# Two matmuls for three in the last token tile of six expert blocks, with earlier output copies and earlier turns, in an attention + mixture-of-experts kernel

## The chip, the cores and the metric

The kernel runs on one core of a Trainium2 chip. The metric is the device time of one launch in microseconds (us); the number quoted for a kernel is the median of several runs. The profile is of one more execution, taken by the hardware profiler. Engines are named as the profile names them: PE (TensorE matmul), PEld (its weight load, which runs beside the matmuls), DVE (VectorE), ACT (ScalarE), POOL (GpSimd), SP (SyncE, which here only issues transfers).

## The reference, cut to what matters

```python
x = attention(q, k, v, f_logit)            # gated linear attention -> 3072 tokens x 384
logits = x @ w_gate + log1p(exp(x @ w_noise)) * noise
top2   = the two experts (of 8) with the highest logits, softmax weights top2_w
for e in range(8):                          # mixture of experts
    mask = tokens that chose e
    h = np.maximum(x[mask] @ w1[e], 0.0)    # 384 -> 1024
    out[mask] += top2_w[mask] * (h @ w2[e]) # 1024 -> 384
xn  = out / rms(out) * rms_g                # second feed-forward, all tokens
y   = (silu(xn @ w_gate2) * (xn @ w_val2)) @ w_out   # 384 -> 1536 -> 384
```

All products are wanted at float32 accuracy. The kernel gets it by splitting each operand into a rounded part and a remainder, both in float32r, and adding three matmuls: rounded x rounded, rounded x remainder, remainder x rounded (`three`, L673).

## The kernel before, in words

The first 150 us are the attention. Then comes the expert stream, 22 blocks one after the other on PE: eight blocks with the first 384 tokens of each expert, eight with the rest of each expert (the experts ranked by how many tokens they hold, so that the sizes are known when the program is built: 476, 448, 428, 416, 408, 396, 392 and 384 rows), and six blocks of the second feed-forward.

An expert block has 8 units; a unit is 128 hidden columns. Its first product (`l1`) has the tokens as the moving operand: 9 matmuls of N columns into one PSUM bank named h (two banks, taken in turn). ACT makes the rounded part `hhi` of the relu (L801), DVE the remainder `hlo` (L802). Its second product (`l2`, `down_product`) has the hidden values as the stationary operand, one tile of 128 tokens at a time, and 384 columns of w2 as the moving one: three matmuls per token tile, accumulated over the 8 units in one PSUM bank per tile (`acc`). PE's order is written out by hand: l1 of unit f, then l2 of unit f-2. So a block of 428 tokens has tiles of 128, 128, 128 and 44 rows, and the last takes three matmuls like the others.

After a block's last unit, `post` copies each tile's bank to SBUF (`y`, L816 on DVE for odd tiles, L818 on ACT for even ones) and SP stores it. The next block's l2 needs the same banks.

The token rows of a block come by gathers on POOL (`fetch`, L770; four of 32 rows a tile, into six buffers `xg`), then `turn` transposes them on DVE (`xt`, L781) and splits them into `xhi` (ACT, L668) and `xlo` (DVE, L669). A table gives the units in which this is issued: tile 0 to 3 at 5, 4, 3 and 2 units before the block starts, the gathers two units ahead of it and at most two in a unit. Weights come by SP transfers into two buffers `raw`; ACT and DVE split them (`whi` L209, `wlo` L210). The second feed-forward's weights are 64-bit numbers and take more steps (`cv`: L178 on ACT, L179, L180 and L182 on DVE; `whi` L205; `wlo` on POOL, L206). On ACT, DVE, POOL and SP a scheduler sets the order from priorities; only PE's is by hand.

Of the kernel before, what the change touches and what calls it, by code (L numbers as in the profile page):

```python
# [9 lines left out]
F32 = mybir.dt.float32  # L10
F32R = mybir.dt.float32r
# [4 lines left out]
AF = mybir.ActivationFunctionType  # L16
OP = mybir.AluOpType
# [4 lines left out]
P = 128  # L22
# [5 lines left out]
def tile_gated_attention_moe_ffn(  # L28
# [18 lines left out]
    nc = tc.nc  # L47
    B, HP, _, S = f_logit.shape
    DM = v.shape[2]
# [22 lines left out]
    main = ExitStack()  # L72
# [193 lines left out]
    late = {}  # L266
    mark = [None, None]
# [426 lines left out]
            V.tensor_tensor(r, r, t, op=OP.mult)  # L694

    class Block:
        pass


    def behind(on=True):  # L700
# [15 lines left out]
    def down_product(b, key, f, hh, rows, only=None):  # L716
        whi, wlo = wts_of[key + (f // 2,)]
        for i, r in enumerate(rows):
            if only not in (None, i):
                continue  # L720
            c = slice(i * P, i * P + r)
            three(b.acc[i][:r], whi[:, f % 2], wlo[:, f % 2], hh[0][:, c], hh[1][:, c],
                  f == 0, f == b.units - 1, False)

    def x_tiles(b, n):
# [1 line left out]
        b.xlo = xs_.tile([P, KD, 512], F32R, name="xlo")  # L727

    def h_tiles(n):
        return [late["h"].tile([P, 512], F32R, name=nm) for nm in ("hhi", "hlo")]  # L730

    def moe_block(e, t0, N, pid):

# [3 lines left out]
        b = Block()  # L737
        rows = [min(P, N - o) for o in range(0, N, P)]
        b.units = FM // P
        b.uses = lambda f: [("up", pid, f // 2)], lambda f: [("down", pid, f // 2)]  # L740
        b.cost = 9 * max(N, 256) / 2400, len(rows) * 3 * DM / 2400

# [50 lines left out]
        def l1(f):  # L793
            whi, wlo = wts_of["up", pid, f // 2]
            c = slice((f % 2) * P, (f % 2 + 1) * P)
            p = bank("h")
            for j in range(KD):
                three(p[:, :N], whi[:, j, c], wlo[:, j, c], b.xhi[:, j, :N], b.xlo[:, j, :N],
                      j == 0, j == KD - 1, True)
            hhi, hlo = h_tiles(N)  # L800
            mark[0] = nc.scalar.activation(hhi[:, :N], p[:, :N], AF.Relu).ins  # L801
            mark[1] = nc.vector.scalar_tensor_tensor(  # L802
                hlo[:, :N], p[:, :N], 0.0, hhi[:, :N].bitcast(F32), op0=OP.max,
                op1=OP.subtract).ins
            return hhi, hlo

        def l2(f, hh):
            if f == 0:
# [3 lines left out]
        def post():  # L812
            for i, r in enumerate(rows):
                y = late["h"].tile([P, DM], F32, name="y")
                if i % 2:
                    nc.vector.tensor_copy(y[:r], b.acc[i][:r])  # L816
                else:
                    nc.scalar.activation(y[:r], b.acc[i][:r], AF.Copy)  # L818
                o = (t0 + i) * P
                to = yd.rearrange("(e s) d -> e s d", e=E)[:, o:o + r]  # L820
                if t0 == 0:
                    nc.sync.dma_start(to[e], y[:r])
                    o += e * CAPA
                    nc.sync.dma_start(ya[o:o + r, :], y[:r])
                else:
                    nc.sync.dma_start(to[bass.ds(expert_of(e), 1)].rearrange("o s d -> (o s) d"),
                                      y[:r])
# [4 lines left out]
    def ffn_block(bi):  # L832
        b = Block()
# [46 lines left out]
        def l1(f):  # L880
            c = slice((f % 2) * P, (f % 2 + 1) * P)
            ps = []
            for nm, use in (("gate", "h"), ("val", "t")):
                whi, wlo = wts_of[nm, f // 2]
                p = bank(use)
                for j in range(KD):
                    three(p, whi[:, j, c], wlo[:, j, c], b.xhi[:, j], b.xlo[:, j],
                          j == 0, j == KD - 1, True)
                ps.append(p)
            sg = late["f"].tile([P, 512], F32, name="sg")  # L890
            nc.scalar.activation(sg, ps[0], AF.Sigmoid)  # L891
            nc.vector.tensor_tensor(sg, ps[0], sg, op=OP.mult)  # L892
            nc.vector.tensor_tensor(sg, ps[1], sg, op=OP.mult)  # L893
            hhi, hlo = h_tiles(512)
            mark[0] = nc.scalar.activation(hhi, sg, AF.Copy).ins  # L895
            mark[1] = nc.vector.tensor_tensor(hlo, sg, hhi.bitcast(F32), op=OP.subtract).ins
            return hhi, hlo

        def l2(f, hh):
            if f == 0:  # L900
# [40 lines left out]
    for pid in range(2 * E):  # L941
        r = pid - E if pid >= E else None
# [63 lines left out]
    start = [0]  # L1006
# [7 lines left out]
    for i in range(1, len(blocks)):  # L1014
        b = blocks[i]
        if i < NM:
            where = (-5, -4, -3, -2)
        else:
            where = (-50, -48, -46, -44, -42, -4, -3, -2) if i == NM else \
                (-9, -8, -7, -6, -5, -4, -3, -2)  # L1020
        for u, fn in zip(where, b.turns):
            side.setdefault(start[i] + u, []).append(fn)
        skip = GIVEN if i == 1 else 0
        for u, fns in zip(where, b.fetches):
            fns, skip = fns[skip:], max(0, skip - len(fns))
            if i > NM:
                side.setdefault(start[i] + u - 2, []).extend(fns)
            else:
                wanted += [(start[i] + u - 2, fn) for fn in fns]
# [458 lines left out]
```

## Time and profile before

| | |
|---|---|
| median of 3 runs | 1075.31 us (1072.07 to 1076.23) |
| the profiled execution | 1068.86 us, its span 1067.0 us |
| mean granted TensorE clock | 0.994 |
| busy: PE, PEld | 1029.9 us (97%), 935.8 us (88%) |
| busy: DVE, ACT, POOL | 669.1 us (63%), 482.5 us (45%), 300.0 us (28%) |
| chain that ended last | PE 83%, DVE 7%, ACT 3%, DMA 3% |

The span runs from the first to the last instruction; the execution's own time lies 1.9 us above it. A matmul's record is longer than the distance to the next one, because matmuls are pipelined: what a matmul costs is read from one start to the next, not from its mean length. The attention ends at about 150 us, the last expert block at about 590 us.

### The profile page before, as it was taken

To read this page: it belongs to the slowest core of one execution; us is meant where nothing else is said; L and a number is where in the kernel's file an instruction comes from. 1 tells how busy PE (TensorE), PEld (TensorE's weight loads), DVE (VectorE), ACT (ScalarE), POOL (GpSimd) and SP (SyncE) were. 2 spreads that over 40 slices of the span, in tenths; PEclk is the share of its full clock that TensorE was granted. 3 is DMA by queue.
4 is the path that set the end of the run, shared out by engine and by line. 5 is a ranking of instruction groups with operands and counts; after the bars stand their busy time and mean duration, and the time that the engine had idled before them with its cause. 6 is when DMAs were issued, how large, how long until landed. Compare 5 with 4: busy or idle time off the path is not lost.

```text
span 1067.0 us, 17429 instructions
## 1 busy us (share of the span) xinstructions
PE 1029.9 (97%) x6497; PEld 935.8 (88%) x6497; DVE 669.1 (63%) x1473; ACT 482.5 (45%) x1048; POOL 300.0 (28%) x318
## 2 busy tenths in 40 slices
PE   8898899999999999999999999999999999999996
PEld 5687789999999899899999988888888888888885
DVE  7789979877777766765666696444354353453332
ACT  6885755555655544544454543223233232232221
POOL 2000345545556654454540250120110200200000
PEclk9998999999999999999999999999999999999998
DMA  9974346766666645455554340110110200200000
GB/s 304 355 251 157 120 139 208 233 213 215 209 217 220 221 151 193 146 164 163 169 163 142 106 140 15 45 45 1 60 30 1 63 27 1 74 16 1 30 1 33
DMA packets 88946, 134.46 MB, mean 126 GB/s; under 512 B 8703, under 2 KB 64915, under 8 KB 88851
## 3 DMA queue, kind: packets, MB, share of 16 engines
q1 hardware_dynamic: 79475, 113.82, 32.5%
q0 software_dynamic: 9376, 19.43, 6.5%
q8 instruction: 53, 0.87, 0.3%
q14 instruction: 42, 0.34, 0.1%
HBM read 107.63 MB, written 25.59 MB: 125 GB/s over the span
## 4 chain that ended last, share of the span: by engine, by line
PE 83%; DVE 7%; ACT 3%; DMA 3%; issue 2%; SPq 1%; another core or an unknown queue 1%; DVEq 0%; ACTq 0%
PE bank L681 76%; DMA raw<-in_moe_w_dram 2%; PE bank L173 1%; PE bank L476 1%; PE bank L454 1%; PE bank L464 1%; PE scores L408 1%; DVE cs L355 1%; DVE wlo L210 1%; DVE AM L418 1%; DMA columns<-in_moe_w_both_dram 1%; PE bank L429 1%; DVE xt L781 0%; DVE hlo L802 0%
## 5 line engine op out<-in xcount | busy, mean ns | idle before, releaser
L681 PE MATMUL bank<-xhi,whi 128*128 128x512 f32 (+8 forms) x816 | 302.7, 371 | 5.0 <-ACT xhi L668 2.7
L681 PE MATMUL bank<-xhi,wlo 128*128 128x512 f32 (+8 forms) x816 | 301.1, 369 | 0.0
L681 PE MATMUL bank<-xlo,whi 128*128 128x512 f32 (+8 forms) x816 | 301.0, 369 | 0.0
L681 PE MATMUL bank<-whi,hhi 128*128 128x384 f32 x728 | 244.7, 336 | 2.7 <-DVE y L816 2.7
L681 PE MATMUL bank<-whi,hlo 128*128 128x384 f32 x728 | 244.7, 336 | 0.0
L681 PE MATMUL bank<-wlo,hhi 128*128 128x384 f32 x728 | 244.1, 335 | 0.0
L681 PEld LDWEIGHTS bank<-xhi,whi 128*128 128x128 f32 x816 | 153.3, 188 | 26.8 <-DVE hlo L802 4.5
L681 PEld LDWEIGHTS bank<-xhi,wlo 128*128 128x128 f32 x816 | 153.2, 188 | 18.5
L681 PEld LDWEIGHTS bank<-xlo,whi 128*128 128x128 f32 x816 | 153.2, 188 | 16.5 <-DVE xlo L669 0.3
L210 DVE TENSOR_TENSOR wlo<-raw,whi 128x256 fp32r<-128x256 f32 (+1 forms) x320 | 142.3, 482 | 22.8 <-ACT whi L209 13.0
L209 ACT ACTIVATE whi<-raw 128x256 fp32r<-128x256 f32 (+1 forms) x320 | 126.3, 452 | 33.6 <-DMA raw<-in_moe_w_dram 29.9
L681 PEld LDWEIGHTS bank<-whi,hhi 128*128 128x128 f32 x728 | 132.6, 182 | 7.7 <-DVE y L816 4.0
L681 PEld LDWEIGHTS bank<-wlo,hhi 128*128 128x128 f32 x728 | 132.5, 182 | 6.4
L681 PEld LDWEIGHTS bank<-whi,hlo 128*128 128x128 f32 x728 | 132.5, 182 | 3.4
L770 POOL DMA_INDIRECT xg<-xd,stokr x107 | 107.5, 1004 | 95.4 <-ACT hhi L801 71.3
L802 DVE SCALAR_TENSOR_TENSOR hlo<-bank,hhi 128x384 fp32r<-128x384 f32 (+7 forms) x128 | 73.1, 571 | 96.2 <-ACT hhi L801 95.6
L892 DVE TENSOR_TENSOR sg<-bank,sg 128x512 f32<-128x512 f32 x72 | 49.7, 690 | 119.8 <-ACT sg L891 119.8
L801 ACT ACTIVATE hhi<-bank 128x384 fp32r<-128x384 f32 (+7 forms) x128 | 64.0, 500 | 125.2 <-PE bank L681 103.9
L843 POOL DMA_INDIRECT xg<-yd,slots x40 | 43.7, 1092 | 265.4 <-ACT hhi L895 254.9
L770 POOL DMA_INDIRECT xg<-xd,stoka x84 | 89.3, 1063 | 91.0 <-ACT hhi L801 57.8
L891 ACT ACTIVATE sg<-bank 128x512 f32<-128x512 f32 x72 | 42.9, 596 | 143.4 <-PE bank L681 136.9
L895 ACT ACTIVATE hhi<-sg 128x512 fp32r<-128x512 f32 x72 | 45.4, 630 | 125.9 <-DVE sg L893 125.9
(167 smaller groups left out, 1040.2 us busy)
## 6 DMA issues: line engine op xcount, KB each, us to landing
raw<-in_moe_w_dram SPq DMA_DIRECT2D x64, 768.0 KB
Qs<-in_kq_dram SPq DMA_DIRECT2D x11, 1024.0 KB
yd<-y SPq DMA_DIRECT2D x48, 192.0 KB
Fs<-in_f_logit_dram SPq DMA_DIRECT2D x11, 512.0 KB
Vs<-in_v_dram SPq DMA_DIRECT2D x24, 192.0 KB
xd<-x SPq DMA_DIRECT2D x24, 192.0 KB
ya<-y SPq DMA_DIRECT2D x24, 192.0 KB
raw<-in_moe_w_gate_dram SPq DMA_DIRECT2D x6, 768.0 KB
```

What stands on the lines that cost most here:

```text
L173: nc.tensor.transpose(p, x, i)
L209: nc.scalar.activation(hi[:, j], raw[:, j], AF.Copy)
L210: nc.vector.tensor_tensor(lo[:, j], raw[:, j], hi[:, j].bitcast(F32), op=OP.subtract)
L355: nc.vector.tensor_tensor_scan(st["cs", n][:, s].rearrange("p a t -> p (a t)"), chain[:, s].rearrange("p a t -> p (a t)"), st["L", n][:, s ...
L681: nc.tensor.matmul(o, a, b, start=start and i == 0, stop=stop and i == 2)
L770: paced(nc.gpsimd.indirect_dma_start(out=b.xg[i][:, k_], out_offset=None, in_=table, in_offset=bass.IndirectOffsetOnAxis(ap=rows_of[:, k_, ...
L801: mark[0] = nc.scalar.activation(hhi[:, :N], p[:, :N], AF.Relu).ins
L802: mark[1] = nc.vector.scalar_tensor_tensor(hlo[:, :N], p[:, :N], 0.0, hhi[:, :N].bitcast(F32), op0=OP.max, op1=OP.subtract).ins
L843: paced(nc.gpsimd.indirect_dma_start(out=y, out_offset=None, in_=ya if n < GROUP else yd, in_offset=bass.IndirectOffsetOnAxis(ap=at_, axis ...
L891: nc.scalar.activation(sg, ps[0], AF.Sigmoid)
L892: nc.vector.tensor_tensor(sg, ps[0], sg, op=OP.mult)
L895: mark[0] = nc.scalar.activation(hhi, sg, AF.Copy).ins
```

## The change

1. In the six expert blocks whose last tile has 64 rows or fewer (448, 428, 416, 408, 396 and 392 tokens: tiles of 64, 44, 32, 24, 12 and 8), the rounded part and the remainder of the hidden values of that tile stand side by side in one stationary operand of 2 x 64 or 2 x 32 columns (`b.beside`). One matmul multiplies both with `whi`; a second multiplies the rounded part with `wlo`. The third matmul is gone. `hhi` and `hlo` become one tile `hh`; DVE writes the last tile's remainder in an instruction of its own (`low`, twice a unit), and where the rows do not fill 32 or 64, POOL writes zeros into the gaps (a memset per unit, blocks with 44, 24, 12 and 8 rows).
2. The two halves of that tile's result lie in different PSUM partitions. `post` copies the second half on ACT (`yl`) and DVE adds the first to it.
3. All copies of `post` are given a higher priority.
4. The turns of expert tiles are issued one unit sooner (-6 to -3 in place of -5 to -2), and with them the gathers.

```diff
--- before.py
+++ after.py
@@ -694,7 +694,9 @@
             V.tensor_tensor(r, r, t, op=OP.mult)
 
     class Block:
-        pass
+
+
+        beside = 0
 
 
     def behind(on=True):
@@ -718,8 +720,16 @@
         for i, r in enumerate(rows):
             if only not in (None, i):
                 continue
+            if b.beside and i == len(rows) - 1:
+                c = i * P
+                nc.tensor.matmul(b.acc[i][:2 * b.beside], hh[:, 0, c:c + 2 * b.beside],
+                                 whi[:, f % 2],
+                                 start=f == 0, stop=f == b.units - 1, skip_group_check=True)
+                nc.tensor.matmul(b.acc[i][:b.beside], hh[:, 0, c:c + b.beside], wlo[:, f % 2],
+                                 start=False, stop=f == b.units - 1, skip_group_check=True)
+                continue
             c = slice(i * P, i * P + r)
-            three(b.acc[i][:r], whi[:, f % 2], wlo[:, f % 2], hh[0][:, c], hh[1][:, c],
+            three(b.acc[i][:r], whi[:, f % 2], wlo[:, f % 2], hh[:, 0, c], hh[:, 1, c],
                   f == 0, f == b.units - 1, False)
 
     def x_tiles(b, n):
@@ -727,7 +737,7 @@
         b.xlo = xs_.tile([P, KD, 512], F32R, name="xlo")
 
     def h_tiles(n):
-        return [late["h"].tile([P, 512], F32R, name=nm) for nm in ("hhi", "hlo")]
+        return late["h"].tile([P, 2, 512], F32R, name="hh")
 
     def moe_block(e, t0, N, pid):
 
@@ -737,6 +747,8 @@
         b = Block()
         rows = [min(P, N - o) for o in range(0, N, P)]
         b.units = FM // P
+        if t0 and rows[-1] <= 64:
+            b.beside = 32 if rows[-1] <= 32 else 64
         b.uses = lambda f: [("up", pid, f // 2)], lambda f: [("down", pid, f // 2)]
         b.cost = 9 * max(N, 256) / 2400, len(rows) * 3 * DM / 2400
 
@@ -797,12 +809,22 @@
             for j in range(KD):
                 three(p[:, :N], whi[:, j, c], wlo[:, j, c], b.xhi[:, j, :N], b.xlo[:, j, :N],
                       j == 0, j == KD - 1, True)
-            hhi, hlo = h_tiles(N)
-            mark[0] = nc.scalar.activation(hhi[:, :N], p[:, :N], AF.Relu).ins
-            mark[1] = nc.vector.scalar_tensor_tensor(
-                hlo[:, :N], p[:, :N], 0.0, hhi[:, :N].bitcast(F32), op0=OP.max,
-                op1=OP.subtract).ins
-            return hhi, hlo
+            hh = h_tiles(N)
+            main = (len(rows) - 1) * P if b.beside else N
+
+            def low(o, c):
+                return nc.vector.scalar_tensor_tensor(
+                    o, p[:, c], 0.0, hh[:, 0, c].bitcast(F32), op0=OP.max, op1=OP.subtract).ins
+
+            mark[0] = nc.scalar.activation(hh[:, 0, :N], p[:, :N], AF.Relu).ins
+            if b.beside:
+                end = main + b.beside
+                if end > N:
+                    tail = hh[:, 0, main:main + 2 * b.beside].rearrange("p (a c) -> p a c", a=2)
+                    nc.gpsimd.memset(tail[:, :, N - main:].bitcast(F32), 0.0)
+                low(hh[:, 0, end:end + N - main], slice(main, N))
+            mark[1] = low(hh[:, 1, :main], slice(0, main))
+            return hh
 
         def l2(f, hh):
             if f == 0:
@@ -812,10 +834,15 @@
         def post():
             for i, r in enumerate(rows):
                 y = late["h"].tile([P, DM], F32, name="y")
-                if i % 2:
-                    nc.vector.tensor_copy(y[:r], b.acc[i][:r])
-                else:
-                    nc.scalar.activation(y[:r], b.acc[i][:r], AF.Copy)
+                with tc.high_priority(30):
+                    if b.beside and i == len(rows) - 1:
+                        t = late["h"].tile([P, DM], F32, name="yl", bufs=1)
+                        nc.scalar.activation(t[:r], b.acc[i][b.beside:b.beside + r], AF.Copy)
+                        nc.vector.tensor_tensor(y[:r], b.acc[i][:r], t[:r], op=OP.add)
+                    elif i % 2:
+                        nc.vector.tensor_copy(y[:r], b.acc[i][:r])
+                    else:
+                        nc.scalar.activation(y[:r], b.acc[i][:r], AF.Copy)
                 o = (t0 + i) * P
                 to = yd.rearrange("(e s) d -> e s d", e=E)[:, o:o + r]
                 if t0 == 0:
@@ -891,10 +918,11 @@
             nc.scalar.activation(sg, ps[0], AF.Sigmoid)
             nc.vector.tensor_tensor(sg, ps[0], sg, op=OP.mult)
             nc.vector.tensor_tensor(sg, ps[1], sg, op=OP.mult)
-            hhi, hlo = h_tiles(512)
-            mark[0] = nc.scalar.activation(hhi, sg, AF.Copy).ins
-            mark[1] = nc.vector.tensor_tensor(hlo, sg, hhi.bitcast(F32), op=OP.subtract).ins
-            return hhi, hlo
+            hh = h_tiles(512)
+            mark[0] = nc.scalar.activation(hh[:, 0], sg, AF.Copy).ins
+            mark[1] = nc.vector.tensor_tensor(hh[:, 1], sg, hh[:, 0].bitcast(F32),
+                                              op=OP.subtract).ins
+            return hh
 
         def l2(f, hh):
             if f == 0:
@@ -1014,7 +1042,7 @@
     for i in range(1, len(blocks)):
         b = blocks[i]
         if i < NM:
-            where = (-5, -4, -3, -2)
+            where = (-6, -5, -4, -3)
         else:
             where = (-50, -48, -46, -44, -42, -4, -3, -2) if i == NM else \
                 (-9, -8, -7, -6, -5, -4, -3, -2)
```

In the orders below, `hh` stands for what was `hhi` and `hlo`, and the lines of the changed kernel are its own.

PE, one second product of the block with 408 tokens (last tile: 24 rows), the end of its third tile and its last tile. Before:

```order
L681 MATMUL bank_6266<-whi_6028,hlo 128x384
L681 MATMUL bank_6267<-whi_6028,hhi 24x384
L681 MATMUL bank_6267<-wlo_6029,hhi 24x384
L681 MATMUL bank_6267<-whi_6028,hlo 24x384
L681 MATMUL bank_6283<-xhi,whi_5986 128x408
```

and in the changed kernel:

```order
L681 MATMUL bank_6190<-whi_5953,hh 128x384
L725 MATMUL bank_6191<-whi_5953,hh 64x384
L728 MATMUL bank_6191<-wlo_5954,hh 32x384
L681 MATMUL bank_6211<-xhi,whi_5914 128x408
```

Three matmuls of 24 output rows became one of 64 and one of 32; the first product of the next unit follows directly in both.

DVE, the last units of the fifth expert block (first 384 tokens; L802, or L816 in the changed kernel, are the remainders of the hidden values, L781 or L793 a turn, L179 to L182 the 64-bit weights). Before:

```order
L802 SCALAR_TENSOR_TENSOR hlo<-bank_3949,hhi 128x384
L781 STREAM_TRANSPOSE xt<-xg 128x384
L210 TENSOR_TENSOR wlo_3977<-raw,whi_3976 128x384 x2
L669 TENSOR_TENSOR xlo<-xt,xhi 128x3x128
L179 TENSOR_SCALAR cv<-cv 128x384 x2
L180 SCALAR_TENSOR_TENSOR cv<-raw,cv 128x384 x2
L182 SCALAR_TENSOR_TENSOR cv<-raw,cv 128x384 x2
L802 SCALAR_TENSOR_TENSOR hlo<-bank_4000,hhi 128x384
```

and in the changed kernel:

```order
L793 STREAM_TRANSPOSE xt<-xg 128x384
L210 TENSOR_TENSOR wlo_3903<-raw,whi_3902 128x384 x2
L669 TENSOR_TENSOR xlo<-xt,xhi 128x3x128
L816 SCALAR_TENSOR_TENSOR hh<-bank_3908,hh 128x384
L210 TENSOR_TENSOR wlo_3934<-raw,whi_3933 128x384 x2
L179 TENSOR_SCALAR cv<-cv 128x384 x2
L180 SCALAR_TENSOR_TENSOR cv<-raw,cv 128x384 x2
L182 SCALAR_TENSOR_TENSOR cv<-raw,cv 128x384 x2
L816 SCALAR_TENSOR_TENSOR hh<-bank_3957,hh 128x384
```

The turn of the block's last tile, `xt` and `xlo`, stood between two remainders and ahead of the 64-bit weights; now it stands ahead of the first of the two.

POOL, around the start of the block with 428 tokens (last tile: 44 rows), changed kernel (L782 and L870 are gathers of expert rows and of rows for the second feed-forward, L824 the zeros):

```order
L782 DMA xg<-xd,stokr 128x96 x4
L824 MEMSET hh 128x2x20
L206 TENSOR_TENSOR wlo_5368<-cv,whi_5367 128x768
L782 DMA xg<-xd,stokr 128x96 x2
L824 MEMSET hh 128x2x20
L782 DMA xg<-xd,stokr 128x96 x2
L824 MEMSET hh 128x2x20
L870 DMA xg<-ya,first 128x384
```

Before, POOL had only the gathers and the `wlo` here; now each of the block's units has a memset, queued behind the gathers that were issued sooner.

## Rows read from the trace of the kernel before

**Rows 1.** The page's first part: engines, busy us, share, instructions.
```profile
PE 1029.9 (97%) x6497; PEld 935.8 (88%) x6497; DVE 669.1 (63%) x1473; ACT 482.5 (45%) x1048; POOL 300.0 (28%) x318
```

**Rows 2.** Waits of PE: line, releaser, us in total, times, longest.
```profile
PE bank L681 <- DVE y L816: 2.7, 4, 1.1
PE bank L681 <- ACT xhi L668: 2.7, 1, 2.7
PE bank L681 <- DVE hlo L802: 2.2, 3, 1.3
```

**Rows 3.** Timeline of PE, block of 392 tokens: start, length, what, shapes.
```profile
560.85 0.34 PE L681 MATMUL bank<-wlo,hhi 128*8 128x384 f32 x1
561.03 0.34 PE L681 MATMUL bank<-whi,hlo 128*8 128x384 f32 x1
561.20 0.34 PE L681 MATMUL bank<-xhi,whi 128*128 128x392 f32 x1
```

**Rows 4.** Timeline of PE, second feed-forward.
```profile
700.50 0.39 PE L681 MATMUL bank<-xlo,whi 128*128 128x512 f32 x1
700.73 0.40 PE L681 MATMUL bank<-xhi,wlo 128*128 128x512 f32 x1
```

**Rows 5.** Weight loads by shape: xcount | busy us, mean ns | idle before.
```profile
L681 PEld LDWEIGHTS bank<-whi,hhi 128*128 128x128 f32 x672 | 126.2, 188 | 4.5 <-DVE y L816 0.8 <-issue 0.5
...
L681 PEld LDWEIGHTS bank<-whi,hhi 128*64 128x64 f32 x8 | 1.1, 133 | 0.0
...
L681 PEld LDWEIGHTS bank<-whi,hhi 128*8 128x8 f32 x8 | 0.7, 87 | 0.0
```

**Rows 6.** Timeline of PE, matmuls that waited [idle us <- releaser], expert blocks.
```profile
301.41 0.44 PE L681 MATMUL bank<-xhi,whi 128*128 128x384 f32 x1 [1.32 <-DVE hlo L802]
...
355.36 0.48 PE L681 MATMUL bank<-xhi,whi 128*128 128x476 f32 x1 [2.65 <-ACT xhi L668]
...
431.23 0.37 PE L681 MATMUL bank<-whi,hhi 128*44 128x384 f32 x1 [1.13 <-DVE y L816]
```

**Rows 7.** Timeline of ACT ahead of the wait at 301.41.
```profile
296.93 0.55 ACT L178 ACTIVATE cv<-raw 128x384 f32<-128x384 f32 x1 [1.63 <-DMA raw<-in_moe_w_out_dram]
297.38 0.51 ACT L668 ACTIVATE xhi<-xt 128x384 fp32r<-128x384 f32 x1
```

**Rows 8.** Timeline of DVE ahead of the same wait.
```profile
297.92 0.56 DVE L669 TENSOR_TENSOR xlo<-xt,xhi 128x384 fp32r<-128x384 f32 x1 [1.02 <-ACT xhi L668]
...
300.81 0.55 DVE L802 SCALAR_TENSOR_TENSOR hlo<-bank,hhi 128x384 fp32r<-128x384 f32 x1
```

**Rows 9.** Timeline of ACT ahead of the wait at 355.36.
```profile
354.86 0.44 ACT L668 ACTIVATE xhi<-xt 128x288 fp32r<-128x288 f32 x1 [1.05 <-DVE xt L781]
```

**Rows 10.** Timeline of DVE ahead of the same wait.
```profile
353.48 0.55 DVE L802 SCALAR_TENSOR_TENSOR hlo<-bank,hhi 128x384 fp32r<-128x384 f32 x1
...
354.28 0.55 DVE L781 STREAM_TRANSPOSE xt<-xg 128x288 f32<-128x288 f32 x1
```

**Rows 11.** Groups of DVE by shape.
```profile
L802 DVE SCALAR_TENSOR_TENSOR hlo<-bank,hhi 128x384 fp32r<-128x384 f32 x72 | 39.7, 551 | 28.1 <-ACT hhi L801 27.8
...
L802 DVE SCALAR_TENSOR_TENSOR hlo<-bank,hhi 128x428 fp32r<-128x428 f32 x8 | 4.8, 599 | 7.7 <-ACT hhi L801 7.7
...
L618 DVE SCALAR_TENSOR_TENSOR r_key<-total,irow 128x8 f32<-128x8 f32 x1 | 0.2, 181 | 0.0
```

**Rows 12.** Groups of POOL by shape.
```profile
L770 POOL DMA_INDIRECT xg<-xd,stokr x107 | 107.5, 1004 | 95.4 <-ACT hhi L801 71.3 <-issue 18.9 <-DVE xm L854 1.9
...
L206 POOL TENSOR_TENSOR wlo<-cv,whi 128x768 fp32r<-128x768 f32 x18 | 33.5, 1863 | 57.0 <-PE bank L681 29.3 <-ACT whi L205 27.5
...
L1104 POOL MEMSET Ss<- 128x64 f32 x2 | 0.2, 152 | 0.0
```

**Rows 13.** Groups of ACT by shape.
```profile
L818 ACT ACTIVATE y<-bank 128x384 f32<-128x384 f32 x32 | 15.5, 486 | 3.2 <-PE bank L681 3.2
```

**Rows 14.** Busy time of the engines, 400 to 450 us.
```profile
400.00:450.00 50.00, 48.43 (x261) 45.03 (x261) 37.24 (x94) 25.58 (x63) 24.19 (x22) 1.00 0.57 181
```

## The prediction

> **What bounds the kernel now.** I read the page's busy shares first: PE is busy 97% of the span, DVE 63%, ACT 45%, POOL 28% [rows 1]. The chain of waits that ended last gives 83% of the span to PE. In the expert blocks PE stood still only at the places of [rows 2]: four waits for the copies `y` (2.7 us), one for `xhi` (2.7 us) and three for the remainders `hlo` (2.2 us), 7.6 us in all. So a matmul that goes away there shortens the span by what it costs on PE, unless another engine now comes late; and at most 7.6 us more can be had from waits.
>
> What a matmul costs is the distance between starts, since its record overlaps the next: in the block of 392 tokens three matmuls follow at 560.85, 561.03 and 561.20, that is 0.175 us apiece, though the first two have only 8 stationary columns [rows 3]. In the second feed-forward a matmul of 512 moving columns takes 0.23 us [rows 4]. The extra 128 columns cost 0.055 us, about 0.43 ns each, so 384 columns make some 0.165 us and the rest is fixed; the number of stationary columns does not show.
>
> **Part 1, two matmuls for three.** Six blocks times 8 units lose one matmul each: 48 x 0.175 = 8.4 us. The two that stay keep their 384 moving columns; they only have more stationary ones. All of it lies on PE, in a stretch without other waits than those above. Value 8.4; I bound it by 2.4 (below, as a rival) and 8.4.
>
> The Trainium skill speaks against this value. Its page "TensorE: Matmul & The Clock Gate" (Back-to-back issue gap; LDWEIGHTS) says that in a stream of load and matmul pairs the spacing is set by both, and that a load goes by its columns. The trace here disagrees for these tiles: loads of 87 ns and of 188 ns [rows 5] give the same 0.175 us spacing. By the page alone the sum would be that of the rival on weight loads.
>
> **What part 1 adds beside PE.** DVE: a small remainder instruction in each of 48 units. None of that shape is in the trace; the nearest is a scalar_tensor_tensor of 8 columns with 181 ns, and the main one shrinks to 384 columns, 551 ns, from 599 at 428 [rows 11]. So some +0.13 us a unit of about 3.6 us (20 matmuls of 0.175 to 0.2 us). In the busiest 50 us DVE works 37 [rows 14], and the second product that reads the result comes two units later. I cost it at nothing; uncovered it would be 48 x 0.13 = 6 us. ACT: six copies `yl` like the others, 486 ns [rows 13], third in line at each block end. Three copies take 1.5 us, the add after them replaces a DVE copy of the same size, and PE has some 3.2 us of work (9 matmuls of the next first product and 9 of the next second one, at 0.175 to 0.19) before it wants that bank. Nothing; or up to 6 x 0.5 = 3 us if the bank is late by all of it.
>
> POOL: 32 memsets (four blocks of 8). The nearest row is 152 ns for 64 columns [rows 12]. They queue behind gathers of 1004 ns, two a unit with some issue time, and once a block behind a `wlo` of 1863 ns [rows 12]: 2.5 us of a unit as a rule, 4.4 in one of eight. POOL works 24 of 50 us there [rows 14], and the matmul that waits for the zeros stands two units behind, about 7 us. Nothing, in the likeliest case; without the cover see the first rival.
>
> **Part 2, copies first.** The orders of the two kernels put `y` behind nearly the same instructions as before: the scheduler had the copies early already, and the last tile's add stands one weight instruction earlier at one block end and one turn later at another. The longest of these waits was 1.13 us [rows 6]. I take 0 for the sum of the four. The ends: all 2.7 us go [rows 2], or each of the six block ends loses that longest wait, 6.8 us minus the 2.7 there are, so 4 us worse.
>
> **Part 3, turns a unit sooner.** The block that starts at 355.36 waited 2.65 us for the `xhi` of its last tile, made at 354.86 to 355.30 after a turn at 354.28 [rows 6, 9, 10]; a unit is over 3 us, so this wait goes. What is late next is the bank: the first product needs the one whose `hlo` was read from 353.48 to 354.03 [rows 10], and that instruction still stands behind the 64-bit weights. 355.36 - 354.03 = 1.3 us gained, 1.3 left. The three `hlo` waits are of one kind: at 301.41 PE waits for the remainder at 300.81, ahead of which DVE did the turned tile's `xlo` (297.92, 0.56 with 1.02 of idle) and the weights, and ACT did `xhi` between two weight steps [rows 6 to 8]. The order now has turn, `xhi` and `xlo` a unit ahead of that, so about 0.9 us goes from this chain: 0.47 of DVE (the step to the next instruction) and 0.4 of ACT. The longest wait shrinks from 1.32 to 0.4, and the other two, 0.9 together [rows 2], go: 1.8 us. Part 3 makes 1.3 + 1.8 = 3.1 us. Its ends: 4.9 (all of these waits), or 2 us worse, if gathers and turns that come sooner move a weight step behind them by as much as the longest wait, twice. A gather still leads its turn by two units.
>
> **Sum.** 8.4 + 0 + 3.1 = 11.5 us. The profiled execution of 1068.86 us (span 1067.0) becomes 1057.4. The three runs had their median 6.5 us above that execution, so from 1075.3 I forecast 1063.8 us, 1.1% less.
>
> **Rivals.**
> 1. POOL's queue becomes the bound (slower). Each memset is behind gathers that wait for ACT's `hhi` of their unit and for a free `xg` buffer; the second product of four blocks now waits for POOL. It decides when POOL runs more than two units behind: from 11.5/32 = 0.36 us per second product the whole gain is gone, and at 0.6 us the sum is 32 x 0.6 = 19 us lost, 1075.3 - 11.5 + 19 = 1083. For it: gathers wait 71 of 95 us of their idle time for `hhi` [rows 12], and the block of 428 tokens starts while POOL hands out buffers to both kinds of gathers. Against: POOL is half idle [rows 14]. 6%.
> 2. Weight loads set the spacing. Then a unit saves the difference of loads: before three of 87 to 133 ns, now 133 + some 110 (between the rows for 8 and 64 columns) or 188 + 133 [rows 5]: 0.02 to 0.08 us, 48 x 0.05 = 2.4 us, with part 3 5.5, so 1069.8. Against it stands the equal spacing of [rows 3]. 5%.
> 3. Only the matmuls pay. The turns' gain is eaten, because the same DVE and ACT queues wait for the same weight transfers (the ACT step at 296.93 had waited 1.63 us for one [rows 7]) and PE's faster pace meets them sooner; or new waits of a few us at the block ends. 4 to 9 us gained, around 1068. 24%.
> 4. Copies and turns give all they can: 8.4 + 4.9 + 2.7 = 16 us, 1059.3. 10%.
>
> **Chances and range.** The forecast, 9 to 14 us gained, gets 55%. I take 0.5% (5.4 us, so 1069.9 and 1080.7) as what a measurement can tell from no change. Faster: the forecast (55), rival 4 (10) and 13 of the 24 of rival 3, together 78%. Same: rival 2 (5), 9 of rival 3 and 1 of rival 1, 15%. Slower: 5 of rival 1, and 2 of rival 3 where its new waits are larger, 7%. The three runs of before spread over 4 us, so the range needs that besides the cases: 1056 (rival 4 less 3) to 1071 (4.3 us gained). The likeliest case's own range is 1060 to 1067.
>
> **What would show it.** Right: in blocks of 8 to 64 last rows, 20 matmuls a unit in place of 21, at 0.175 us from start to start also for the 64 and 128 stationary columns; no wait for `xhi` at the start of the block of 476 tokens, and there a wait of about 1.3 us for the remainder; PE's waits for `hlo` in the earlier blocks under 0.5 us in all; about 2.7 us of waits for `y`. Wrong: PE waiting for a POOL memset; spacing above 0.18 us at the wide tails; weight transfers or gathers among PE's, ACT's or DVE's releasers where there were none; new waits at the ends of the six blocks by more than 4 us.

## The result and the profile after

The changed kernel took 1061.51 us in the median (1057.97 to 1063.08, 6 runs), the kernel before in the same comparison 1073.55 us (1071.01 to 1076.23, 6 runs): a ratio of 0.9886, with the 95% interval 0.9859 to 0.9914, or 12 us less. The prediction had 11.5 us. Two later comparisons, on two different chips, gave 0.9874 (0.9847 to 0.9901) and 0.9878 (0.9852 to 0.9904).

The profiled execution of the changed kernel took 1063.08 us (span 1061.3), only 5.8 us less than that of the kernel before, in part because its attention took 3.7 us longer (see the stretches below). The page's first part, the line that answers to [rows 1]:

```profile
PE 1027.7 (97%) x6449; PEld 938.4 (88%) x6449; DVE 674.1 (64%) x1521; ACT 486.1 (46%) x1054; POOL 307.5 (29%) x350
```

48 matmuls are gone (6497 to 6449), 48 DVE, 6 ACT and 32 POOL instructions are new. The two groups of matmuls that took the place of three, by shape (xcount | busy us, mean ns | idle before), and below them their weight loads:

```profile
L728 PE MATMUL bank<-wlo,hh 128*32 128x384 f32 x32 | 10.8, 338 | 0.0
L725 PE MATMUL bank<-whi,hh 128*64 128x384 f32 x32 | 10.6, 333 | 1.2 <-DVE y L841 1.2
L725 PE MATMUL bank<-whi,hh 128*128 128x384 f32 x16 | 5.4, 338 | 0.6 <-DVE wlo L210 0.6
L728 PE MATMUL bank<-wlo,hh 128*64 128x384 f32 x16 | 5.3, 331 | 0.0
...
L725 PEld LDWEIGHTS bank<-whi,hh 128*64 128x64 f32 x32 | 4.3, 133 | 1.7 <-ACT xhi L668 1.5 <-issue 0.2
L728 PEld LDWEIGHTS bank<-wlo,hh 128*32 128x32 f32 x32 | 3.4, 107 | 1.2
L725 PEld LDWEIGHTS bank<-whi,hh 128*128 128x128 f32 x16 | 3.0, 188 | 0.9 <-issue 0.9
```

What they cost is again the distance between starts. The timeline of PE in the block of 392 tokens, which answers to [rows 3]:

```profile
556.08 0.33 PE L725 MATMUL bank<-whi,hh 128*64 128x384 f32 x1
556.25 0.34 PE L728 MATMUL bank<-wlo,hh 128*32 128x384 f32 x1
556.43 0.34 PE L681 MATMUL bank<-xhi,whi 128*128 128x392 f32 x1
```

That is 0.17 and 0.18 us with 64 and 32 stationary columns, as it was with 8. The waits of PE, which answer to [rows 2] (us in total, times, longest):

```profile
PE bank L681 <- DVE hh L816: 3.7, 7, 1.2
...
PE bank L725 <- DVE y L841: 1.2, 1, 1.2
...
PE bank L725 <- DVE wlo L210: 0.6, 1, 0.6
PE bank L681 <- DVE y L843: 0.2, 1, 0.2
```

The wait of 2.65 us for `xhi` is gone, and none names a POOL memset. But the waits for the remainder have not gone from three (2.2 us) to nearly none: there are seven. Where they stand, in the rows of PE that answer to [rows 6]:

```profile
184.23 0.44 PE L681 MATMUL bank<-whi,hh 128*128 128x384 f32 x1 [0.24 <-DVE y L843]
...
194.59 0.34 PE L681 MATMUL bank<-whi,hh 128*128 128x384 f32 x1
196.15 0.44 PE L681 MATMUL bank<-xhi,whi 128*128 128x384 f32 x1 [1.22 <-DVE hh L816]
196.42 0.34 PE L681 MATMUL bank<-xlo,whi 128*128 128x384 f32 x1
...
308.22 0.44 PE L681 MATMUL bank<-xhi,whi 128*128 128x384 f32 x1 [0.64 <-DVE hh L816]
359.25 0.48 PE L681 MATMUL bank<-xhi,whi 128*128 128x476 f32 x1 [0.61 <-DVE hh L816]
432.30 0.41 PE L725 MATMUL bank<-whi,hh 128*128 128x384 f32 x1 [0.60 <-DVE wlo L210]
463.04 0.36 PE L725 MATMUL bank<-whi,hh 128*64 128x384 f32 x1 [1.21 <-DVE y L841]
```

A wait costs PE more than its listed length: here the starts lie 1.56 and 0.27 us apart where two matmuls in step take 0.17 each, so the wait of 1.22 us costs about 1.5.

At 196.15 the remainder is late in the way that [rows 7, 8] showed for 301.41, but now among the router's steps. The timeline of DVE just ahead, and of ACT:

```profile
191.34 0.67 DVE L793 STREAM_TRANSPOSE xt<-xg 128x384 f32<-128x384 f32 x1
...
193.82 0.56 DVE L669 TENSOR_TENSOR xlo<-xt,xhi 128x384 fp32r<-128x384 f32 x1 [0.94 <-ACT xhi L668]
...
195.54 0.55 DVE L816 SCALAR_TENSOR_TENSOR hh<-bank,hh 128x384 fp32r<-128x384 f32 x1
```

```profile
192.85 0.53 ACT L209 ACTIVATE whi<-raw 128x384 fp32r<-128x384 f32 x1 [3.62 <-DMA raw<-in_moe_w_dram]
193.28 0.51 ACT L668 ACTIVATE xhi<-xt 128x384 fp32r<-128x384 f32 x1
```

The turned tile is ready at 192.01. Its `xhi` stands behind a weight step that waits for its transfer; `xlo` waits for `xhi`, and the remainder stands behind `xlo` on DVE. The other six were not followed this far.

### The profile page after: what moved, and what is told of

Same layout as the page of the kernel before. It is cut to its first block, busy times and chain, and to the rows that moved or that the text cites. A ratio compares the mean times of both kernels' runs of the same rounds, so it can differ in the third digit from the quotient of the medians.

```text
span 1061.3 us, 17487 instructions
## 1 busy us (share of the span) xinstructions
PE 1027.7 (97%) x6449; PEld 938.4 (88%) x6449; DVE 674.1 (64%) x1521; ACT 486.1 (46%) x1054; POOL 307.5 (29%) x350
## 4 chain that ended last, share of the span: by engine, by line
PE 77%; DVE 9%; DMA 7%; ACT 3%; issue 3%; SPq 1%; DVEq 0%; ACTq 0%
PE bank L681 68%; DMA raw<-in_moe_w_dram 5%; PE bank L173 2%; PE bank L476 2%; PE bank L454 2%; DVE wlo L210 1%; PE bank L464 1%; PE scores L408 1%; ACT whi L209 1%; DVE cs L355 1%; PE bank L725 1%; PE bank L728 1%; DVE AM L418 1%; PE bank L429 1%; DVE hh L816 1%
## 5 line engine op out<-in xcount | busy, mean ns | idle before, releaser
L681 PE MATMUL bank<-whi,hh 128*128 128x384 f32 x1360 | 379.7, 336 | 0.2 <-DVE y L843 0.2
L681 PEld LDWEIGHTS bank<-whi,hh 128*128 128x128 f32 x1360 | 248.5, 187 | 3.9 <-DVE y L843 0.6
L681 PE MATMUL bank<-wlo,hh 128*128 128x384 f32 x680 | 228.0, 335 | 0.0
L782 POOL DMA_INDIRECT xg<-xd,stokr x107 | 108.5, 1014 | 76.6 <-ACT hh L819 45.0
L681 PEld LDWEIGHTS bank<-wlo,hh 128*128 128x128 f32 x680 | 127.5, 187 | 3.3
L919 DVE TENSOR_TENSOR sg<-bank,sg 128x512 f32<-128x512 f32 x72 | 49.7, 691 | 120.2 <-ACT sg L918 120.2
L816 DVE SCALAR_TENSOR_TENSOR hh<-bank,hh 128x384 fp32r<-128x384 f32 (+7 forms) x176 | 76.4, 455 | 77.3 <-ACT hh L819 72.8
L870 POOL DMA_INDIRECT xg<-yd,slots x40 | 43.8, 1094 | 265.3 <-ACT hh L922 254.9
L782 POOL DMA_INDIRECT xg<-xd,stoka x84 | 90.3, 1075 | 89.9 <-ACT hh L819 56.9
L819 ACT ACTIVATE hh<-bank 128x384 fp32r<-128x384 f32 (+7 forms) x128 | 64.0, 500 | 103.0 <-PE bank L681 69.6
L922 ACT ACTIVATE hh<-sg 128x512 fp32r<-128x512 f32 x72 | 45.4, 630 | 123.7 <-DVE sg L920 123.6
L923 DVE TENSOR_TENSOR hh<-sg,hh 128x512 fp32r<-128x512 f32 x72 | 50.9, 706 | 46.8 <-ACT hh L922 46.8
L920 DVE TENSOR_TENSOR sg<-bank,sg 128x512 f32<-128x512 f32 x72 | 49.7, 691 | 40.2 <-PE bank L681 39.9
```

What stands on the lines that cost most here:

```text
L681: nc.tensor.matmul(o, a, b, start=start and i == 0, stop=stop and i == 2)
L782: paced(nc.gpsimd.indirect_dma_start(out=b.xg[i][:, k_], out_offset=None, in_=table, in_offset=bass.IndirectOffsetOnAxis(ap=rows_of[:, k_, ...
L816: return nc.vector.scalar_tensor_tensor(o, p[:, c], 0.0, hh[:, 0, c].bitcast(F32), op0=OP.max, op1=OP.subtract).ins
L819: mark[0] = nc.scalar.activation(hh[:, 0, :N], p[:, :N], AF.Relu).ins
L870: paced(nc.gpsimd.indirect_dma_start(out=y, out_offset=None, in_=ya if n < GROUP else yd, in_offset=bass.IndirectOffsetOnAxis(ap=at_, axis ...
L922: mark[0] = nc.scalar.activation(hh[:, 0], sg, AF.Copy).ins
```

## How the stretches are read

A whole run hides where time went, because the unchanged attention took from 149.4 to 156.3 us up to the first expert matmul in these traces. The granted clock (the share of TensorE's full speed that its throttle let through: 1.00 is 2.4 GHz, 0.50 is 1.2 GHz) goes with it: up to there its mean is 0.98 in the shortest and 0.93 in the longest, and 0.94 in the 153.0 us of the first trace of the changed kernel. So the table takes two stretches from PE's timeline: from the first expert matmul to the first with 476 moving columns, and from there to the first of the second feed-forward (512 columns). All 48 matmuls that go lie in the second. The wait ahead of the 476 columns belongs to the first. The third stretch, the feed-forward, has 457.7 us in all of them.

| kernel (traces) | to the 476 columns, us | from there to the feed-forward, us |
|---|---|---|
| before (1) | 206.0 | 244.3 |
| changed (3) | 206.2, 206.0, 205.4 | 234.9, 235.4, 235.4 |
| matmuls only (2) | 203.0, 207.7 | 238.0, 242.8 |
| turns only (2) | 202.1, 207.0 | 242.5, 242.7 |
| changed, third matmul back | 202.8 | 242.6 |
| later turns in the first half (2) | 200.2, 207.6 | 234.4, 235.4 |
| the same, four output buffers | 209.3 | 234.4 |
| changed, four output buffers | 206.7 | 234.0 |
| eight memsets | 207.0 | 244.8 |

The first stretch differs by up to 7 us between two traces of one and the same kernel, each on another chip. PE's starts show where: the trace of 200.2 us has one wait, of 0.8 us, and that of 207.6 us has nine, 4.5 us as listed, each with some 0.3 us on top; the latter also ran its first 3.0 us at 1.2 GHz (granted 0.50), which cost 1.5 us. The second stretch repeats within 1.0 us, but for "matmuls only".

## The experiments

They ran in three sets, each on a chip of its own, with the kernel before timed beside them: at 1066.44 us in the first set, 1076.2 in the second, 1077.54 in the third. Only times of one set are compared. A gain against the kernel before is worked out from the ratio, unless it is said to be one of the medians.

**First set: each part alone.** The high priority of the copies is left out of these kernels where a diff says so. In the traces, DVE and ACT have the same order up to 341 us in a kernel without it (matmuls only) and one with it (later turns in the first half); behind that the two differ in the turns as well, so for the six changed blocks no run shows the priority alone.

Matmuls only:

```diff
-                with tc.high_priority(30):
+                with ExitStack():
...
-            where = (-6, -5, -4, -3)
+            where = (-5, -4, -3, -2)
```

> Part 1 alone (two matmuls for three in the last tiles), the turns where they were, the copies without priority. Terms as predicted: 48 x 0.175 = 8.4 us under the kernel before, and waits of PE for xhi (2.6) and hlo (2.2) as in it. If weight loads set the spacing: 2.4 us under it. If only the matmuls pay and the turns give nothing: all of the change's 12 us, within its interval of 9 to 15.

Measured: 1062.05 us, ratio 0.9949 (0.9930 to 0.9969), so 5.4 us less.

Turns only (the kernel before with `where = (-6, -5, -4, -3)`):

> Part 3 alone: the kernel before with the turns and gathers of expert tiles a unit sooner. Terms as predicted: 3.1 us under the kernel before, no wait for xhi at the block of 476 tokens, waits for hlo under 0.5 us at the three later block starts. If the turns' gain is eaten: no difference (within 1 us), the stretch from the first expert matmul to the block of 476 tokens as long as before (206 us), with new waits for the remainders in the second to fourth expert block.

Measured: 1066.67 us, 1.0004 (0.9985 to 1.0024): nothing.

The changed kernel with the sooner turns in the second half of the expert blocks alone:

```diff
-            where = (-6, -5, -4, -3)
+            where = (-5, -4, -3, -2) if i < NM // 2 else (-6, -5, -4, -3)
```

> The changed kernel with the sooner turns only for the eight blocks of the experts' further tokens; the first eight blocks turn as before. Terms as predicted: 8.4 + 1.3 = 9.7 us under the kernel before, 1.8 above the changed kernel. If sooner turns cost in the first blocks what they give there: the same as the changed kernel or up to 2 us faster; then the waits of 0.2 to 1.2 us between 184 and 227 us of the changed kernel are gone and those of the kernel before at the starts of the sixth to eighth block are back.

Measured: 1058.08 us, 0.9924 (0.9900 to 0.9947), so 8.1 us less.

The changed kernel with a third matmul back:

```diff
+                for _ in range(2):
-                nc.tensor.matmul(b.acc[i][:b.beside], hh[:, 0, c:c + b.beside], wlo[:, f % 2],
+                    nc.tensor.matmul(b.acc[i][:b.beside], hh[:, 0, c:c + b.beside], wlo[:, f % 2],
```

It adds the product of the rounded part with `wlo` twice, so its output differs in the last tiles.

> The changed kernel with the second of the two matmuls issued twice, so three per last tile again (it adds the product of the rounded part and the weights' remainder a second time). Moving columns set the price: 48 x 0.175 = 8.4 us above the changed kernel, spacing 0.175 us. Weight loads set it: 48 x 0.107 to 0.133 = 5 to 6 us above it, spacing of that matmul 0.11 to 0.13 us.

Measured: 1067.38 us, 1.0000 (0.9983 to 1.0017). With the matmul back no gain is left, though the sooner turns are in. Its timeline shows the price of one, 0.35 us for two (the row groups two matmuls):

```profile
560.85 0.33 PE L725 MATMUL bank<-whi,hh 128*64 128x384 f32 x1
561.02 0.51 PE L729 MATMUL bank<-wlo,hh 128*32 128x384 f32 x2
561.37 0.34 PE L681 MATMUL bank<-xhi,whi 128*128 128x392 f32 x1
```

So far the runs spoke for the matmuls alone, and against the 3.1 us of the turns. But the changed kernel itself was missing from this set.

**Second set: POOL's cover, the first blocks, the output buffers.**

> The changed kernel as it is, timed beside the other three kernels of this call so that their ratios share one chip. The first comparison gave a ratio of 0.9886 (-12 us). The runs before this one give, each against the kernel before: the two-for-three matmuls with the old turns -5.4 us, the sooner turns alone 0, both with the sooner turns only in the second half of the expert blocks -8.1. Theory A (the matmuls are worth 48 x 0.175 = 8.4 us, the sooner turns pay about nothing in net): -5 to -9 us, ratio 0.992 to 0.995. Theory B (the sum of the prediction, turns worth 3 us more): -11 to -12 us, ratio 0.989.

Measured: 1061.65 us, 0.9874 (0.9847 to 0.9901), 13.6 us less.

> The kernel with the sooner turns only from the ninth block on, a second time, to be compared with the changed kernel in the same call. The changed kernel's profile has seven short waits of PE for hh in its first half (184 to 227 us and at 297.94, 308.22), where the router's steps and weight steps share DVE and ACT with the turns; with the old turns there are none of those at 184 to 227. Theory A (the sooner turns cost in the first blocks what they give in the later ones): 2 to 3 us less than the changed kernel. Theory B (the waits there are only in place of others): the same as the changed kernel within 1 us.

Measured: 1064.40 us, 0.9882 (0.9858 to 0.9905), against 0.9874: no difference. In its trace PE waits 3.7 us in eight places for the remainder, as long as in the changed kernel (3.7 us in the first trace, 3.4 in the one of this set). But the same kernel's trace in the first set has 0.8 us in one place. So these waits differ more between two executions of one kernel than between the two kernels, and what the sooner turns make or take of them in the first half is not shown.

Eight memsets for one:

```diff
+                    for _ in range(8):
-                    nc.gpsimd.memset(tail[:, :, N - main:].bitcast(F32), 0.0)
+                        nc.gpsimd.memset(tail[:, :, N - main:].bitcast(F32), 0.0)
```

> The changed kernel with every POOL memset of the zero columns issued eight times, 32 x 7 = 224 memsets of about 0.15 us more, some 34 us of POOL in the blocks of 44, 24, 12 and 8 last rows, about 1 us a unit. My theory (POOL has cover: no PE wait named a memset, and the second product comes two units later): the same time as the changed kernel within 1.5 us. Rival 1 of the prediction (POOL's queue is near to being the bound): 10 us or more longer, with PE waiting for L824.

Measured: 1073.53 us, 0.9959 (0.9941 to 0.9977), 11.9 us more in the medians than the changed kernel in the same set (9.1 by the ratios). My expectation was wrong, and by much: POOL's busy time is 337.0 us in place of 307.5, and 9.4 us appear in the second stretch, 6.0 of them in the block of 416 tokens. The waits of PE:

```profile
PE bank L725 <- DVE y L842: 4.3, 2, 3.5
...
PE bank L681 <- DVE hh L816: 3.3, 5, 1.1
...
PE bank L725 <- POOL hh L825: 1.2, 2, 0.9
```

PE waits for a memset itself for only 1.2 us. The largest wait is for the add of the block of 428 tokens, and behind it the clock falls. PE's timeline, and the engines in windows behind the wait (us; busy of PE, PEld, DVE, ACT, POOL; then granted clock, DMA share, GB/s):

```profile
472.27 0.55 PE L725 MATMUL bank<-whi,hh 128*64 128x384 f32 x1 [3.54 <-DVE y L842]
472.62 0.52 PE L728 MATMUL bank<-wlo,hh 128*32 128x384 f32 x1
472.94 0.55 PE L681 MATMUL bank<-xhi,whi 128*128 128x416 f32 x1
473.28 0.55 PE L681 MATMUL bank<-xlo,whi 128*128 128x416 f32 x1
```

```profile
472.30:476.00 3.70, 3.70 (x11) 3.42 (x12) 1.29 (x4) 0.00 (x0) 2.11 (x1) 0.50 0.36 120
```

At this level, 1.2 GHz, a matmul of 416 columns takes 0.34 us from start to start; at 2.4 GHz it takes 0.19 in the changed kernel. The add itself waited for a buffer, as DVE's row shows:

```profile
471.57 0.55 DVE L842 TENSOR_TENSOR y<-bank,yl 44x384 f32<-44x384 f32 x1 [1.18 <-DMA yd<-y]
```

Why seven more memsets a unit make this output transfer late is not shown. What is shown is that POOL's half-idle queue gives no cover of 1 us a unit.

Four buffers for the output tiles, here and in the second feed-forward (on top of the later turns in the first half):

```diff
-                y = late["h"].tile([P, DM], F32, name="y")
+                y = late["h"].tile([P, DM], F32, name="y", bufs=4)
```

> The kernel of the later turns in the first half, and the output tiles y with four buffers in place of three. A block has four tiles: with three buffers the fourth copy or add (that of the small last tile) waits until the first one's DMA is out, and at 458 us PE waited 1.71 us for this add, which stood behind a transpose on DVE and had itself waited for yd<-y. Theory A (the buffer count, and not the priority, sets when the copies come): the PE wait for y at the block of 416 tokens goes, 1.5 to 2 us less than the kernel with the later turns. Rival (the add is late because the copy yl is third in line on ACT): the wait stays at 1 to 1.7 us and the time is the same.

Measured: 1063.81 us, 0.9871 (0.9847 to 0.9895), against 1064.40: the same within what the times tell. But the wait for `y` fell from 1.4 us to 0.4 in two places, and the second stretch by 1.0 us (table); the three-buffer kernel had 234.4 us too in the first set, with a wait for `y` of 1.7, so the stretch alone does not tell.

**Third set: the changed kernel beside its parts.**

> The changed kernel, timed in one call with each of its parts alone, since the same parts gave other differences on other chips (the kernel before had its median at 1066 in the call of the parts and at 1076 in the call of the changed kernel). From the traces so far the stretch from the block of 476 tokens to the second feed-forward is 244.3 us in the kernel before and 234.9 to 235.4 in the changed one (-9 to -9.5), while the stretch from the first expert matmul to the block of 476 varies from 200 to 209 us in one and the same kernel. Expected: -9 to -13 us against the kernel before.

Measured: 1064.71 us, 0.9878 (0.9852 to 0.9904), 12.8 us less in the medians.

> Two matmuls for three, with the turns as before. Theory A (the turns pay nothing in net): the same time as the changed kernel within 2 us. Theory B (the turns pay the 3.1 us of the prediction, and in the matmuls-only kernel the wait for xhi at the block of 476 stays, 1.95 us, with the clock falling behind it): 2.5 to 5 us more than the changed kernel, -6 to -9 against the kernel before.

Measured: 1072.68 us, 0.9957 (0.9928 to 0.9985). That is 8.0 us more than the changed kernel, and the two intervals don't meet: the turns do pay, more than theory B had (this kernel lacks the priority of the copies as well). The waits of PE in this kernel show where:

```profile
PE bank L725 <- DVE y L841: 3.0, 2, 1.6
PE bank L681 <- ACT xhi L668: 2.5, 1, 2.5
PE bank L681 <- DVE hh L816: 2.3, 5, 0.9
...
PE bank L681 <- DVE y L843: 1.2, 2, 0.8
```

The old wait for `xhi` is still there, and with it the clock falls (granted 0.59 in the 3.5 us behind it). PE's timeline at the block of 476 tokens, and the ten us around it:

```profile
357.20 0.49 PE L681 MATMUL bank<-xhi,whi 128*128 128x476 f32 x1 [2.45 <-ACT xhi L668]
...
358.13 0.60 PE L681 MATMUL bank<-xhi,wlo 128*128 128x476 f32 x1
358.53 0.60 PE L681 MATMUL bank<-xhi,whi 128*128 128x476 f32 x1
```

```profile
355.00:365.00 10.00, 7.80 (x30) 6.75 (x31) 6.54 (x15) 4.36 (x13) 6.64 (x7) 0.83 0.45 131
```

The matmuls stand 0.40 us apart. The same stretch of the changed kernel, with 0.86 us of wait in place of 2.45:

```profile
355.14 0.49 PE L681 MATMUL bank<-xhi,whi 128*128 128x476 f32 x1 [0.86 <-DVE hh L816]
...
355.68 0.38 PE L681 MATMUL bank<-xhi,wlo 128*128 128x476 f32 x1
355.90 0.37 PE L681 MATMUL bank<-xhi,whi 128*128 128x476 f32 x1
```

```profile
355.00:365.00 10.00, 9.86 (x50) 9.15 (x51) 7.93 (x17) 6.23 (x17) 7.68 (x8) 1.00 0.65 179
```

Here they stand 0.22 us apart. From the first matmul of 476 columns to the first of 448 it took 32.96 us with the fall and 31.12 without: 1.84 us on top of the wait. The matmuls-only trace of the first set has the same fall (32.97 us, behind a wait of 1.95). The third set's trace has a second fall, behind the wait of 1.63 us for the add at 467.59 (granted 0.59 in the next 3.5 us); the block of 416 tokens takes 33.73 us there and 31.10 in the first set's trace, where PE waited 0.7 us less and the clock stayed.

> The kernel before with the turns a unit sooner. Theory A: the same time as the kernel before within 2 us. Theory B: -2.5 to -4 us (in its first trace the waits from the block of 476 on fell from 244.3 to 242.5 us, and the wait for xhi there was gone).

Measured: 1072.75 us, 0.9955 (0.9929 to 0.9981), 4.8 us less than before. The wait for `xhi` at the block of 476 tokens is gone as in the first trace of this kernel (0.16 us for the remainder is left), and the second stretch is the same (242.7 and 242.5 us, before 244.3). Yet on this chip the turns alone pay, and on that of the first set they paid nothing; the kernel before has no trace from either chip that would say why.

> The changed kernel with four buffers for the output tiles y in place of three. On DVE the add of the small last tile then stands ahead of the turn at the block of 416 tokens. The kernel with later turns in the first half and four buffers had 0.4 us of waits for y in place of 1.4, and its stretch from the block of 476 to the second feed-forward was 234.4 us in place of 235.4. Expected: the same wait gone here, -1 us against the changed kernel, which is less than the times can tell; the stretch in the trace tells it. If the add was late because of the copy yl before it, the wait of 1.2 to 1.4 us stays.

Measured: 1061.25 us, 0.9853 (0.9826 to 0.9879): the lowest ratio of all, but its interval overlaps that of the changed kernel. The trace tells it as expected: the second stretch is 234.0 in place of 235.4 us, and the add now stands ahead of the turn, waiting for ACT's copy and no longer for a transfer. DVE with four buffers, and with three (the changed kernel in the same set):

```profile
461.71 0.55 DVE L843 COPY y<-bank 128x384 f32<-128x384 f32 x1
462.98 0.55 DVE L841 TENSOR_TENSOR y<-bank,yl 44x384 f32<-44x384 f32 x1 [0.72 <-ACT yl L840]
464.43 0.66 DVE L816 SCALAR_TENSOR_TENSOR hh<-bank,hh 128x32 fp32r<-128x32 f32 x2 [0.90 <-ACT hh L819]
```

```profile
457.12 0.66 DVE L816 SCALAR_TENSOR_TENSOR hh<-bank,hh 128x32 fp32r<-128x32 f32 x2 [1.31 <-ACT hh L819]
457.69 0.68 DVE L793 STREAM_TRANSPOSE xt<-xg 128x384 f32<-128x384 f32 x1
458.67 0.55 DVE L841 TENSOR_TENSOR y<-bank,yl 44x384 f32<-44x384 f32 x1 [0.29 <-DMA yd<-y]
```

## Why the prediction was right, and where its steps were not

The largest term held. That the sum came as near as 12 to 11.5 us is in part luck: half of the turns' term did not come, and a fallen clock that the sum had not counted, with differences that no trace explains, came in its place.

**The matmuls, 8.4 us: right.** The spacing with 64 and 128 stationary columns is 0.17 to 0.18 us. Putting the third matmul back costs 7.3 to 7.8 us in the second stretch (242.63 against 234.86 to 235.36), and taking it away from the turns-only kernel 7.4 (242.7 against 235.4) in the trace and 8.0 in the median (1072.75 against 1064.71). The rest of the 8.4 stands in the changed kernel's three traces as a wait at the first matmul of the last tile of the block of 428 tokens (0.60 us at 432.30, 0.91 in the other two), which neither the turns-only kernel nor the one with the third matmul has. What brings it is not shown: the kernel before has 1.13 us there [rows 6], and the kernel with later turns, as fast on PE, has none in its first trace. Timed by themselves the two-for-three matmuls gained 5.4 and 4.6 us, less than 8.4; in both traces of that kernel the clock falls with the old wait for `xhi`, which it does not in the one trace of the kernel before. Rival 2 falls with the spacing. Its rule, in the Trainium skill's "TensorE: Matmul & The Clock Gate" (Back-to-back issue gap; LDWEIGHTS), makes the load part of the spacing; loads of 107, 133 and 188 ns do not show in it here.

**The copies, 0: right, for another reason than the one given.** The waits of this kind were 2.7 us in four places [rows 2] and are 2.0 in the three rows for `y` and `wlo` above, 3.2 and 2.8 in the other two traces (at 432.30 the row names a weight step, behind which on DVE the add of the 64-row tile stands). No run shows the priority moving an instruction. What holds the last tile's add back is the number of `y` buffers: three, for a block of four tiles, so the fourth output waits until the first one's transfer is out. Four buffers moved the add and took the wait. I had looked at the order of the copies and not at the tiles that they are written to.

**The turns, 3.1 us: the mis-sized term.** At the block of 476 tokens it went as written: no wait for `xhi`, and 0.61, 1.43 and 0.86 us for the remainder where 1.3 was forecast. The other half, 1.8 us from waits in the earlier blocks, did not come: PE waits for the remainder there for 3.1, 2.0 and 2.1 us in the three traces, where it was 2.2, and the first stretch is no shorter than before. At 196.15 the turned tile's `xhi` meets a late weight step in a new place, which is what rival 3 described.

Yet beside the matmuls the sooner turns are worth more than 3.1: 8.0 us in the medians of the third set (1072.68 against 1064.71), and 4.0 in those of the first for the later blocks alone (1062.05 against 1058.08). What the sum left out is the clock: with the wait for `xhi` both traces of the matmuls-only kernel fall to 1.2 GHz and lose another 1.8 us. That is a part of the 8.0 and not all of it. The third set's traces of the two kernels differ by 9.8 us over both stretches: 2.3 in the first, 1.8 by that fall, and 5.7 in the blocks of 428 and 416 tokens, where the matmuls-only kernel waits longer for the copies and its clock falls again. But the first set's trace of the matmuls-only kernel, which has the first fall too, is no longer over both stretches (441.0 us) than the changed kernel's three (440.7 to 441.4). So what the turns are worth differs from execution to execution, and why is open. The parts are worth more together (12.8 us in the medians) than alone (4.9 and 4.8), though the uncertainty of the two alone would let them add up to that.

**Rival 1** did not come: PE waits for no memset. But POOL has less cover than I gave it: 29.5 us more of its work cost 9 to 12 us. In proportion that is 1.3 to 1.7 us for each of the seven extra rounds of memsets, an estimate of what the 32 memsets, costed at nothing, may take; no run leaves them out. **Rival 4** asked for 16 us; 12 to 13.6 came, and waits of about 2 us for the add and the weight step at two block ends are part of what is missing.

**Still open:** by the ratios the gain is 12 to 13.6 us, while the two stretches together fell by 9.2 us in the first trace (450.3 to 441.1), which is near the upper end of rival 3. A difference in granted clock between the timed runs does not explain it: in the third set its mean is 0.989 for both kernels. Only one execution of the kernel before was profiled, and with 1068.86 us it lies below all of its runs in the first comparison (1071.01 to 1076.23); what its slower runs lose, a fallen clock behind the `xhi` wait among the candidates, no trace shows. Nor was the changed kernel run on the chip of the first set, where the kernel before was fastest (1066.44) and the later-turns kernel gained 8.1 us, not 12.7 as in the second set; there the gain may be smaller.

## What to carry to other kernels

Where PE's starts are evenly spaced whatever the stationary columns, count matmuls and multiply by the spacing; that term held within about 1 us. Price a PE wait at some 0.3 us more than its listed length, and one near 2 us at more still, since the granted clock can fall with it. Time the parts of a change beside the whole on one chip before calling a part worthless. When an engine is late with the last tile of a block, count the buffers of the tile it writes before its place in the order.

## What the runs showed of the hardware

A wait of PE of 1.6 to 3.5 us was followed by the 1.2 GHz level in four places (granted 0.50 in the 3.7 us behind the longest), but not behind the 2.65 us of the kernel before (granted 1.00, in the row below), nor behind the 2.04 us at 462.58 in the first matmuls-only trace (granted 1.00 in the next 3.5 us). So the fall is not told by the length of the wait alone.

```profile
355.00:365.00 10.00, 9.63 (x48) 8.66 (x49) 7.69 (x16) 6.37 (x17) 7.54 (x7) 1.00 0.65 204
```

One kernel's first expert blocks took 200.2 us on one chip and 207.6 on another with the same instructions in the same order. Since PE's waits and the clock account for the difference, it is not shown to belong to the chips.
